# A planner's allowance for a DRAM round trip: softmax row sums in a transformer block on one core

## The chip, the cores and the metric

The kernel runs on one core of one Trainium2 chip. The metric is the device time of one execution, in microseconds (us). The kernel before took 1211.61 us as the median of three runs (1210.0 to 1219.1).

Engine names: PE is the matrix engine, PEld its weight loads, DVE the vector engine, ACT the scalar engine, POOL the general engine. SP only issues DMAs in this kernel, and PSUM holds the outputs of its matmuls (`F_ps`, `S_ps`).

## The reference

```python
x = A_x                                   # (1, 2048, 1024), bf16
h  = x + attention(layernorm(x), wq, wk, wv, wo)   # 32 query heads of 32, ONE key/value head
h2 = h + (sigmoid(g) * u) @ w_down                 # g, u = layernorm(h) @ w_gate, @ w_up; F = 3584
return h2
```

There are 16 tiles of 128 tokens. The exponentials of the scores run on ACT (1024 instructions of 1024 columns, 64 for each token tile). The feed-forward network (FFN) of earlier tiles runs on PE at the same time. For each half of the heads of a tile (32 halves in all), the attention output has to be divided by the row sums of the exponentials.

## The kernel before

The kernel does not write its instruction order by hand. A small list scheduler, `Plan`, simulates all engines with estimated durations. It picks the order of every engine's instructions, and then emits those orders with semaphores. What it believes of a DMA is three lines:

```python
# class Plan, step()  (cut)
        self.free[e] = s + o.occ
        o.start = s
        if o.nbytes:
            if o.pace:
                self.pace_free = s + o.nbytes / self.PACE_RATE
            go = max(s + 1300.0, self.dma_free)
            self.dma_free = go + o.nbytes / self.DMA_RATE      # DMA_RATE = 260.0 bytes per ns
            o.end = self.dma_free + 700.0
        else:
            o.end = s + o.lat
        o.pos = len(self.lists[e])
        self.lists[e].append(o)
```

The row sums make a trip. PE sums over the partitions, DVE takes the reciprocal into `r_sb`, SP writes 8 KB to DRAM (`rd`), and SP reads it back spread over the partitions as 256 KB (`rb`). DVE then multiplies (`OT`).

```python
# mk_SUM(hf), after the summing matmuls  (cut)
rc = pl.op("dve", lambda: DVE.reciprocal(r_sb[:, :], F_ps[:, b, 0:64]), [last, rd_ld.get(hf - 1)], ...)
rd_ld[hf] = dma(lambda: SP.dma_start(r_dram, r_sb[0:P:4, :]), "rd", 8192, [rc, rb_ld.get(hf - 1)], prio=0)
rb_ld[hf] = dma(lambda: SP.dma_start(rb[:, :], bass.AP(r_dram.tensor, r_dram.offset, [[512, 4], [0, DH], [1, 512]])),
                "rb", 262144, [rd_ld[hf], ot_ev.get(hf - 1)], prio=0)
# finish(hf)  (cut)
ot_ev[hf] = pl.op("dve", lambda: DVE.tensor_tensor(out=OT[...], in0=o..., in1=rb[...], op=ALU.mult),
                  [oun_ev[(hf, 1)], op_last.get(c - 1), rb_ld[hf]], prio=0, occ=600, lat=690)
if hh == 1:                                   # second half of the heads: the output projection follows
    for dc in range(2):
        queues["OP"].append(mk_OP(c, dc))
```

All FFN, attention-output and projection matmuls share two PSUM banks (`F_ps`). A bank is free again when DVE has emptied it: `hact` for the FFN, `oun` for the attention output, `h_sb` for the residual sums. DVE also adds up all exponentials (`acc`). The FFN's gate half is emptied by a tanh on ACT (`tnh`).

The softmax here doesn't subtract the row's maximum and nothing guards it: scores larger than these inputs give would overflow.

## Time and profile before

| | before |
|---|---|
| median time | 1211.61 us |
| span of the profiled run | 1210.4 us |
| PE busy / idle (span less busy) | 1110.9 / 99.5 us |
| last score matmul / what follows it | 1120.7 us / 89.7 us |
| DVE idle until the returned sums arrive | 66.6 us in 32 waits |
| one token tile in attention (64 exponentials) | about 68.5 us |

These are two lines of the profile's page of the kernel before. The first gives busy time (share of the span) and instructions of each engine, the second the chain of waits by engine.

```profile
...
PE 1110.9 (92%) x15144; PEld 757.5 (63%) x15176; DVE 869.1 (72%) x1076; ACT 1036.2 (86%) x1159; POOL 51.2 (4%) x93
...
PE 53%; DMA 17%; DVE 14%; ACT 9%; issue 6%; SPq 1%; DVEq 0%
...
```

PE is busy 92% of the span. The chain that ended last still runs through DMAs for 17% of it, and nearly all of that is the row sums' trip (13% for the read, 3% for the write).

The next fence is busy time by window, of the stretch with attention and of the tail after the last score matmul. Columns: window, its length, each engine's busy us (instructions), granted PE clock, DMA share, GB/s.

```profile
...
core 0: us, PE busy (x) PEld busy (x) DVE busy (x) ACT busy (x) POOL busy (x), PEclk, DMA share, GB/s
60.00:1120.70 1060.70, 984.42 (x13461) 650.35 (x13489) 791.95 (x911) 991.42 (x1094) 31.41 (x45) 0.99 0.57 172
1120.70:1210.40 89.70, 83.49 (x1130) 74.53 (x1129) 21.52 (x37) 9.02 (x15) 1.34 (x3) 0.98 0.69 209
...
```

With attention running, PE and ACT are each busy about 93% and DVE 75%. In the tail only PE has much to do.

The waits of the kernel before come next. Columns: engine and line, what it waited for, us in total, times, longest.

```profile
...
engine line waited for: us in total, times, longest us
...
DVE OT L652 <- DMA rb<-r_scratch: 66.6, 32, 6.8
...
ACT Pr L601 <- PE S_ps L367: 55.6, 58, 4.1
...
PE F_ps L367 <- DVE hact L884: 24.5, 26, 3.0
...
PE F_ps L367 <- DVE oun L672: 17.6, 17, 2.8
...
```

DVE stood idle for 66.6 us in front of the multiply (line 652) until the read had landed, once in every half of the heads. PE waited for DVE to empty its banks, and ACT waited for scores.

### The profile page before, as it was taken

The numbers are of one execution on the slowest core, as the hardware profiler recorded it, in microseconds if no ns is written. First come the engines' busy times: TensorE is split into PE (matmuls) and PEld (weight loads), VectorE is DVE, ScalarE is ACT, GpSimd is POOL, SyncE is SP. The second block draws the span as 40 slices with busy tenths as digits, with TensorE's granted clock in tenths as the row PEclk, the third lists the DMA queues.
The fourth block names the chain that finished last, engine by engine and source line by source line (L and its number), as shares of the span: only waits on it lengthen the run. The fifth ranks groups of instructions, "written<-read, shape, count | busy, mean of one in ns | idle before, by whom it ended". The sixth has DMA issues, their size and how long they took to land.

```text
span 1210.4 us, 34593 instructions
## 1 busy us (share of the span) xinstructions
PE 1110.9 (92%) x15144; PEld 757.5 (63%) x15176; DVE 869.1 (72%) x1076; ACT 1036.2 (86%) x1159; POOL 51.2 (4%) x93
## 2 busy tenths in 40 slices
PE   6898978889999999999999999989999999999998
PEld 5533455557566665666666675657665675766797
DVE  8996878667786768687786768677776667777321
ACT  3899999889998999999998999989998998999110
POOL 3200000010000100010000100000000000000000
PEclk9899999999999999999999999999999999999999
DMA  9334284774747375664737384655747374664884
GB/s 314 118 96 150 84 263 138 228 228 149 219 129 213 103 230 150 182 197 138 238 115 228 102 251 142 203 171 165 216 134 221 94 214 131 191 192 123 240 261 128
DMA packets 213335, 214.47 MB, mean 177 GB/s; under 512 B 16192, under 2 KB 199488, under 8 KB 213184
## 3 DMA queue, kind: packets, MB, share of 16 engines
q1 hardware_dynamic: 213184, 212.26, 57.8%
q8 instruction: 119, 1.95, 0.7%
q14 instruction: 32, 0.26, 0.1%
HBM read 204.08 MB, written 8.13 MB: 175 GB/s over the span
## 4 chain that ended last, share of the span: by engine, by line
PE 53%; DMA 17%; DVE 14%; ACT 9%; issue 6%; SPq 1%; DVEq 0%
PE F_ps L367 44%; DMA rb<-r_scratch 13%; ACT Pr L601 8%; PE S_ps L367 8%; DVE acc L578 7%; DMA r_scratch<-r_sb 3%; DVE hact L884 2%; DVE oun L672 1%; DVE st L311 1%; SPq L825 1%; DVE st L313 1%; ACT tnh L878 1%; DVE r_sb L636 1%; PE F_ps L755 0%; DVE OT L652 0%
## 5 line engine op out<-in xcount | busy, mean ns | idle before, releaser
L601 ACT ACTIVATE Pr<-S_ps 128x1024 bf16<-128x1024 f32 x1008 | 965.5, 1034 | 63.2 <-PE S_ps L367 55.6
L578 DVE TENSOR_TENSOR acc<-acc,Pr 128x2048 bf16<-128x2048 bf16 x430 | 525.4, 1222 | 49.9 <-ACT Pr L601 30.7
L367 PE MATMUL F_ps<-hnT,ring 128*128 128x128 bf16 x6752 | 438.9, 220 | 21.9 <-DVE hact L884 8.7
L367 PEld LDWEIGHTS F_ps<-hnT,ring 128*128 128x128 bf16 x6752 | 385.1, 98 | 91.4 <-issue 65.5
L367 PE MATMUL F_ps<-zone,hact 128*128 128x256 bf16 x1792 | 225.8, 273 | 3.0 <-DVE hact L884 2.0
L367 PE MATMUL S_ps<-QTb,kT 32*128 32x512 bf16 x2048 | 204.2, 389 | 15.9 <-ACT Pr L601 12.8
L367 PEld LDWEIGHTS F_ps<-zone,hact 128*128 128x128 bf16 x1792 | 163.7, 98 | 47.8 <-issue 22.8
L367 PE MATMUL F_ps<-Pr,Vt 128*32 128x512 bf16 x2016 | 130.2, 387 | 5.7 <-DVE hact L884 5.5
L878 ACT ACTIVATE tnh<-F_ps 128x512 f32<-128x512 f32 x112 | 67.3, 601 | 71.9 <-PE F_ps L367 63.7
L367 PEld LDWEIGHTS S_ps<-QTb,kT 32*128 32x128 bf16 x2048 | 51.6, 91 | 121.4 <-ACT Pr L601 51.1
L884 DVE SCALAR_TENSOR_TENSOR hact<-tnh,F_ps 128x512 bf16<-128x512 f32 x112 | 76.4, 682 | 39.8 <-PE F_ps L367 36.6
L367 PE MATMUL F_ps<-wo_sb,OT 128*128 128x512 bf16 x234 | 67.1, 416 | 28.1 <-DVE hact L884 7.9
L367 PEld LDWEIGHTS F_ps<-Pr,Vt 128*32 128x32 bf16 x2016 | 46.5, 97 | 64.4 <-issue 21.6
L367 PE MATMUL F_ps<-zone 128*128 128x512 bf16 (+3 forms) x574 | 76.5, 282 | 7.1 <-DVE oun L672 2.8
L676 DVE TENSOR_TENSOR oun<-F_ps,oun 128x512 f32<-128x512 f32 x31 | 21.4, 691 | 75.3 <-PE F_ps L367 75.3
L652 DVE TENSOR_TENSOR OT<-oun,rb 128x512 bf16<-128x512 f32 x31 | 21.5, 693 | 65.4 <-DMA rb<-r_scratch 65.4
L367 PEld LDWEIGHTS F_ps<-zone 128*128 128x128 bf16 x584 | 41.2, 102 | 34.3 <-issue 8.3
L367 PEld LDWEIGHTS F_ps<-wo_sb,OT 128*128 128x128 bf16 x256 | 22.6, 103 | 60.7 <-issue 17.8
L324 POOL TENSOR_SCALAR zb<-mvb 128x1 bf16<-128x1 bf16 (+2 forms) x24 | 12.3, 511 | 1092.5 <-DVE mvb L320 1092.4
L920 DVE SCALAR_TENSOR_TENSOR h_sb<-F_ps,h_sb 128x256 bf16<-128x256 f32 x64 | 26.8, 419 | 25.4 <-PE F_ps L367 25.0
L636 DVE RECIPROCAL r_sb<-F_ps 128x64 f32<-128x64 f32 x32 | 17.8, 558 | 26.3 <-PE F_ps L367 26.3
L578 DVE TENSOR_TENSOR acc<-Pr 128x2048 bf16<-128x2048 bf16 x31 | 36.0, 1163 | 0.0
(70 smaller groups left out, 369.5 us busy)
## 6 DMA issues: line engine op xcount, KB each, us to landing
ring<-in_B_w_gate_dram SPq DMA_DIRECT2D x308, 256.0 KB, 3.8
ring<-in_B_w_up_dram SPq DMA_DIRECT2D x308, 256.0 KB, 3.6
rb<-r_scratch SPq DMA_DIRECT2D x32, 256.0 KB
zone<-in_B_w_down_dram SPq DMA_DIRECT2D x14, 512.0 KB, 4.8
Pr<-in_B_w_up_dram SPq DMA_DIRECT2D x20, 256.0 KB, 4.2
Pr<-in_B_w_gate_dram SPq DMA_DIRECT2D x20, 256.0 KB, 4.7
ring<-in_A_x_dram SPq DMA_DIRECT2D x16, 256.0 KB, 6.1
h_sb<-in_A_x_dram SPq DMA_DIRECT2D x16, 256.0 KB, 3.0
```

What stands on the lines that cost most here:

```text
L311: a = pl.op("dve", lambda s=s, src=src: DVE.bn_stats(st[:, s, 0, :], src[:, 0:512]), dp, prio=prio, occ=600, lat=756, order=[st_user.get(s)])
L313: b = pl.op("dve", lambda s=s, src=src: DVE.bn_stats(st[:, s, 1, :], src[:, 512:1024]), dp, prio=prio, occ=600, lat=756, order=[st_user.ge ...
L324: f = pl.op("pool", lambda: POOL.tensor_scalar(out=zb[:, ph, tk], in0=mvb[:, ph, tk, 1], scalar1=LN_EPS_BF16, scalar2=None, op0=ALU.add), ...
L367: return lambda: PE.matmul(o, lhsT=l, rhs=r, start=start, stop=stop, **kw)
L578: add_op[(hf, kt)] = pl.op("dve", lambda: DVE.tensor_tensor(out=a, in0=in0, in1=slot, op=ALU.add), dp, prio=6, **t_dve(2048, 1.92))
L601: exps[u] = pl.op("act", lambda i=i, pb=pb: ACT.activation(out=slot[:, i * 1024:(i + 1) * 1024].rearrange("p (a b) -> p a b", a=2), in_=S_ ...
L636: rc = pl.op("dve", lambda: DVE.reciprocal(r_sb[:, :], F_ps[:, b, 0:64]), [last, rd_ld.get(hf - 1)], prio=0, occ=64 * 8 / 0.96 + 20, lat=6 ...
L652: ot_ev[hf] = pl.op("dve", lambda: DVE.tensor_tensor(out=OT[:, 4 * hh:4 * hh + 4, :], in0=o.rearrange("p (a b) -> p a b", a=4), in1=rb[:, ...
L676: oun_ev[(hf, 1)] = pl.op("dve", lambda: DVE.tensor_tensor(out=o, in0=F_ps[:, b, :], in1=o, op=ALU.add), [last, oun_ev[(hf, 0)]], prio=0, ...
L878: box["a"] = pl.op("act", lambda: ACT.activation(out=tnh[:, :], in_=F_ps[:, b, :], func=ACTF.Tanh, scale=0.5), [last, box.get("e", ot_ev[1 ...
L884: e = pl.op("dve", lambda: DVE.scalar_tensor_tensor(out=ho, in0=shape(tnh[:, :]), scalar=1.0, in1=shape(F_ps[:, b, :]), op0=ALU.add, op1=A ...
L920: e = pl.op("dve", lambda: DVE.scalar_tensor_tensor(out=h_sb[:, t % 4, sl], in0=F_ps[:, b, 0:DW], scalar=0.5, in1=h_sb[:, t % 4, sl], op0= ...
```

## The change

The intent is to tell the planner the truth about the trip, so that it no longer places the multiply on DVE before the sums can be back. The description also named the tanh output and a hold of the first FFN pass. The diff contains nothing of those; this is all of it:

```diff
     ENG = ("act", "dve", "pool", "sp")
     DMA_RATE = 260.0
+    LATE = {"rd": 1500.0, "rb": 3500.0}
     PACE_RATE = 250.0
...
             go = max(s + 1300.0, self.dma_free)
             self.dma_free = go + o.nbytes / self.DMA_RATE
-            o.end = self.dma_free + 700.0
+            o.end = self.dma_free + 700.0 + self.LATE.get(o.key, 0.0)
```

The two numbers shift every later decision of the planner, so the orders of PE, ACT, DVE and SP all change. The set of instructions stays the same, except that three casts move from DVE to ACT and a few weight loads go to other buffers.

## The prediction

> **What the diff is.** Two constants of the planner: the write of the softmax reciprocals to DRAM is assumed to land 1.5 us later, the broadcast read back 3.5 us later. Nothing in it touches the tanh output or a hold on the first FFN pass, which the description names; I predict the diff. By the two instruction orders the work is the same (three casts move from DVE to ACT); only its order on PE, ACT, DVE and SP differs.
>
> **What bounds it now.** Until the last score matmul at 1120.7 us PE and ACT together; then PE alone for 89 us (timeline). In the table of 50 us windows from 300 to 1100 us PE is busy 47 of 50 us, ACT 46.8, DVE 37. Idle between 50 and 1110 us (gaps in the trace): PE 78 us, ACT 69 us.
>
> **The wait aimed at.** From the end of the reciprocal to the multiply that uses the returned sums takes 6.5 to 13 us, once 19 (timeline). The planner allowed about 5 us plus queueing, and DVE keeps its program's order: it stands still for 66.6 us in 32 waits (waits view: OT on rb, at most 6.8 us). Behind it stand the evacuations that free PE's two banks: PE waited 24.5 us for hact and 17.6 us for oun. In the stretches from each such wait to 6 us after its multiply (287 us in all) lie 54.5 of PE's 94 us idle and 56 us of ACT's; at the rate elsewhere PE would have had about 12. So some 42 us of PE idle belong to these waits.
>
> [...]here the small write took 1.7 to 4.4 us to land and the read about 4.7 to 9 us, so the trace decides. The new allowance, about 10 us, matches the measured trip.
>
> **What the new order does.** DVE work between reciprocal and multiply, priced with traced durations, rises from typically 5.4 to 11 us to 10 to 15 us: the 66.6 us of waits should fall under 20 us, ACT's idle from 69 to about 30 us. One token tile (64 exponentials) now takes 68.5 us on average; back to back, ACT needs 62 us (0.92 us spacing, seven tanh at 0.48) and PE is busy 63.6. I expect 65 to 66 us: 15 tiles give back 38 to 52 us.
>
> **What it costs.** The new plan puts less FFN work under attention: after the last score matmul PE has 960 gate/up and 351 down matmuls instead of 729 and 308, an estimated 18 us more at traced spacings (57 and 107 ns). So attention shortens by about 46 us and the tail grows by about 17: net 29 us.
>
> **Prediction: 1182 us**, 1165 to 1203 with 8 in 10. Chances: faster by over 2% 0.62, within 2% 0.35, slower 0.03.
>
> **What would show it.** Right: OT's wait on rb under 20 us; PE's waits on hact and oun halved; last score matmul near 1075 us; tail near 106 us; busy times unchanged within 1%. Wrong, step one: rb waits remain, since the read is issued later on SP, behind paced weight loads. Step two: waits go, but PE's idle returns elsewhere (oun copies now stand right behind the multiply). Step three: the longer tail starves for weights (waits on ring or Pr loads over 5 us).
>
> **What would make it wrong.** PE and ACT are so evenly loaded that relieving one leaves the other's limit: tiles at 67 us would leave about 1205.

The sum is attention shorter by about 46 us and a tail longer by about 17, so 29 us net, from about 1211 to 1182 us. Its traced spacings of 57 and 107 ns are 56 and 109 ns as medians of the tail in the trace of the kernel before.

## More of the kernel before

The timeline shows one such wait in the kernel before. Columns: start, duration, engine, line, operation, output<-inputs, form, count, and in brackets the idle time before it and what ended it.

```profile
...
956.20 0.56 DVE L636 RECIPROCAL r_sb<-F_ps 128x64 f32<-128x64 f32 x1 [2.65 <-PE F_ps L367]
...
956.79 0.49 SPq L638 DMA_DIRECT2D r_scratch<-r_sb  x1
...
960.39 0.55 SPq L639 DMA_DIRECT2D rb<-r_scratch  x1
...
963.58 0.40 PE L367 MATMUL S_ps<-QTb,kT 32*128 32x512 bf16 x4
...
963.91 0.29 PE L367 MATMUL F_ps<-hnT,ring 128*128 128x128 bf16 x2
...
965.45 0.69 DVE L652 TENSOR_TENSOR OT<-oun,rb 128x512 bf16<-128x512 f32 x1 [3.49 <-DMA rb<-r_scratch]
966.06 0.68 DVE L884 SCALAR_TENSOR_TENSOR hact<-tnh,F_ps 128x512 bf16<-128x512 f32 x1
...
966.80 2.79 PE L367 MATMUL F_ps<-hnT,ring 128*128 128x128 bf16 x30 [2.60 <-DVE hact L884]
...
969.52 0.61 PE L367 MATMUL S_ps<-QTb,kT 32*128 32x512 bf16 x4
...
970.06 2.30 PE L367 MATMUL F_ps<-Pr,Vt 128*32 128x512 bf16 x32
...
```

The reciprocal ends at 956.76. The write is issued at once, the read at 960.39, and the multiply starts at 965.45 after DVE has been idle for 3.49 us. Behind the multiply in DVE's order stands `hact`, which empties a bank, so PE idles 2.60 us before 966.80. The last two lines show something that the prediction did not use: the four score matmuls take 0.61 us where they took 0.40 just before. The window of this trouble shows the same in its clock column (next fence, busy time by window of the kernel before: clock 0.97).

```profile
...
950.00:1000.00 50.00, 47.14 (x703) 34.27 (x692) 32.12 (x35) 45.29 (x52) 0.00 (x0) 0.97 0.54 161
...
```

## The result, and the profile after

| | before | after |
|---|---|---|
| median time, the runs when the prediction was made | 1212.76 us (1210.0 to 1219.1) | 1163.85 us (1163.70 to 1163.99) |
| ratio | | 0.959, 95% interval 0.9551 to 0.9628 |
| span of the profiled run | 1210.4 us | 1161.9 us |
| PE idle | 99.5 us | 62.7 us |
| lost to half clock | 19.1 us | 5.1 us |
| last score matmul / tail | 1120.7 / 89.7 us | 1058.4 / 103.5 us |

A ratio is the mean time of one kernel's fast runs over that of the other's fast runs of the same rounds, so it is not quite the ratio of the medians quoted. "Lost to half clock" is half of the time that the trace's clock records show at a granted clock of 0.5. That it is half is an estimate, from the gate and up matmuls of the kernel before: they start every 107 ns at that clock and every 56 elsewhere.

The same two lines of the page of the kernel after:

```profile
...
PE 1099.2 (95%) x15146; PEld 755.7 (65%) x15176; DVE 866.6 (75%) x1073; ACT 1032.4 (89%) x1162; POOL 42.6 (4%) x93
...
PE 79%; DVE 10%; ACT 8%; issue 3%; DMA 0%; DVEq 0%
...
```

The DMAs have left the chain altogether (0%); PE makes up 79% of it.

Busy time by window of the kernel after, the stretch with attention and the tail:

```profile
...
60.00:1058.40 998.40, 957.22 (x13182) 631.29 (x13207) 786.08 (x903) 984.71 (x1093) 22.88 (x45) 1.00 0.59 180
1058.40:1161.90 103.50, 99.17 (x1403) 91.08 (x1403) 24.75 (x43) 11.21 (x18) 1.34 (x3) 1.00 0.69 214
...
```

ACT is now busy 98.6% of the attention stretch, PE 95.9%. The tail is longer because the new order leaves more FFN work for it (1403 matmuls in that window instead of 1130).

The waits of the kernel after (line numbers are one higher):

```profile
...
ACT Pr L602 <- PE S_ps L368: 6.7, 24, 1.4
...
PE F_ps L368 <- DVE hact L885: 4.7, 7, 1.2
...
PE F_ps L368 <- DVE oun L673: 4.0, 8, 0.7
...
DVE OT L653 <- DMA rb<-r_scratch: 0.5, 1, 0.5
...
```

The wait for the sums fell from 66.6 to 0.5 us, PE's waits for `hact` and `oun` fell from 42.1 to 8.7 us, and ACT's wait for scores from 55.6 to 6.7 us.

One trip in the timeline of the kernel after:

```profile
...
874.40 0.56 DVE L637 RECIPROCAL r_sb<-F_ps 128x64 f32<-128x64 f32 x1 [1.12 <-PE F_ps L368]
...
875.62 0.49 SPq L639 DMA_DIRECT2D r_scratch<-r_sb  x1
...
880.96 0.56 SPq L640 DMA_DIRECT2D rb<-r_scratch  x1
...
885.98 0.68 DVE L885 SCALAR_TENSOR_TENSOR hact<-tnh,F_ps 128x512 bf16<-128x512 f32 x1
...
886.43 0.56 PEld L368 LDWEIGHTS F_ps<-hnT,ring 128*128 128x128 bf16 x10 [0.23 <-issue]
...
887.72 0.68 DVE L653 TENSOR_TENSOR OT<-oun,rb 128x512 bf16<-128x512 f32 x1
...
888.07 0.40 PE L368 MATMUL S_ps<-QTb,kT 32*128 32x512 bf16 x4
...
888.40 1.05 PE L368 MATMUL F_ps<-Pr,Vt 128*32 128x512 bf16 x16
...
```

The trip itself has not become shorter: reciprocal to multiply now takes 12.8 us. But DVE has no idle time before the multiply, `hact` runs ahead of it, and the four score matmuls take 0.40 us. Busy time by window, the same 50 us as above: clock 1.00.

```profile
...
950.00:1000.00 50.00, 48.56 (x669) 32.01 (x669) 38.98 (x46) 49.36 (x55) 1.34 (x3) 1.00 0.63 193
...
```

### The profile page after: what moved, and what is told of

Read it like the earlier page. It is cut to its first block, busy times and chain, and to the rows that moved or that the text cites. A ratio compares the mean times of both kernels' runs of the same rounds, so it can differ in the third digit from the quotient of the medians.

```text
span 1161.9 us, 34615 instructions
## 1 busy us (share of the span) xinstructions
PE 1099.2 (95%) x15146; PEld 755.7 (65%) x15176; DVE 866.6 (75%) x1073; ACT 1032.4 (89%) x1162; POOL 42.6 (4%) x93
## 4 chain that ended last, share of the span: by engine, by line
PE 79%; DVE 10%; ACT 8%; issue 3%; DMA 0%; DVEq 0%
PE F_ps L368 66%; PE S_ps L368 12%; ACT Pr L602 8%; DVE acc L579 3%; DVE st L312 1%; DVE st L314 1%; ACT tnh L879 1%; PE F_ps L756 1%; DVE zone L253 1%; DVE r_sb L637 0%; DVE hnT L762 0%; DVE ring L344 0%; DVE oun L673 0%; DVE oun L677 0%; DVE zone L351 0%
## 5 line engine op out<-in xcount | busy, mean ns | idle before, releaser
L368 PE MATMUL S_ps<-QTb,kT 32*128 32x512 bf16 x2048 | 203.1, 387 | 14.7 <-ACT Pr L602 14.2
L368 PEld LDWEIGHTS S_ps<-QTb,kT 32*128 32x128 bf16 x2048 | 51.5, 91 | 121.6 <-ACT Pr L602 56.9
L368 PE MATMUL F_ps<-wo_sb,OT 128*128 128x512 bf16 x236 | 60.6, 381 | 6.3 <-DVE h_sb L921 2.5
L368 PEld LDWEIGHTS F_ps<-zone 128*128 128x128 bf16 x584 | 40.9, 101 | 32.1 <-issue 6.8
L325 POOL TENSOR_SCALAR zb<-mvb 128x1 bf16<-128x1 bf16 (+2 forms) x24 | 6.4, 268 | 1039.1 <-DVE mvb L321 1038.9
L579 DVE TENSOR_TENSOR acc<-Pr 128x2048 bf16<-128x2048 bf16 x31 | 36.1, 1165 | 0.0
L736 DVE TENSOR_TENSOR h_sb<-F_ps,h_sb 128x512 bf16<-128x512 f32 x32 | 22.0, 687 | 9.1 <-PE F_ps L368 8.9
```

Of the source, the lines that this page charges most:

```text
L368: return lambda: PE.matmul(o, lhsT=l, rhs=r, start=start, stop=stop, **kw)
L579: add_op[(hf, kt)] = pl.op("dve", lambda: DVE.tensor_tensor(out=a, in0=in0, in1=slot, op=ALU.add), dp, prio=6, **t_dve(2048, 1.92))
L736: h_ev[(t, dc)] = pl.op("dve", lambda: DVE.tensor_tensor(out=h_sb[:, t % 4, sl], in0=F_ps[:, b, :], in1=h_sb[:, t % 4, sl], op=ALU.add), [ ...
```

## The experiments

Thirteen runs were made: eleven new kernels, and the kernel after and the best of the new ones once more. Each stood beside the kernel before on the same chip. Theory W says that DVE's waits for the sums are the cost. They idle PE and ACT, and PE's idle stretches bring on stretches at half clock (the clock records of the kernel before show a granted clock of 0.5 in eleven stretches of 3.41 us and one that the end of the trace cuts off). Its rival R says that the new orders are better for another reason (less FFN work under attention, or a lucky draw of the planner).

### The wait taken away in the order of the kernel before

```diff
-  in1=rb[:, :].rearrange(...), op=ALU.mult)      # OT
+  in1=o.rearrange(...), op=ALU.mult)             # same work, data already there; wrong result on purpose
...
+  # after planning: OT's dependence on the read is dropped; SP waits for the last read at the end
```

> The order of the kernel before, untouched, but the multiply reads a tile that is already there instead of the returned sums (the result is wrong on purpose; both DMAs still run). Theory W (the waits of DVE for the sums are the cost: they idle PE and ACT, and PE's idle stretches bring on stretches at half clock): no wait on rb, PE's idle between 50 and 1110 us down from 78 to 30-45 us, at most 4 half-clock stretches instead of 12, time 1150 to 1172 us. Rival R (the new order itself is better balanced, it has less FFN work under attention): the waits are worth less than half of the gain, time 1190 to 1210 us.

Measured: 1150.15 us against 1204.91, ratio 0.955 (0.9506 to 0.9594). PE's idle between 50 and 1110 us fell to 29 us, one microsecond below the range expected. Three half-clock stretches were left, at 45 us, at 219 us and in the last microseconds. Busy time by window:

```profile
...
60.00:1062.10 1002.10, 975.36 (x13482) 646.53 (x13481) 789.03 (x910) 986.04 (x1094) 31.48 (x45) 1.00 0.60 182
1062.10:1147.90 85.80, 81.73 (x1131) 73.71 (x1129) 21.44 (x37) 9.00 (x15) 1.34 (x3) 1.00 0.70 218
...
```

The order of the kernel before, with nothing moved, gives slightly more than the whole gain once DVE need not wait. R falls. Its tail is also 17.7 us shorter than that of the kernel after (85.8 against 103.5), so the new order is not better balanced. It costs about 14 us (1164 against 1150), and the change pays that price to be rid of the waits.

The control does the same to the kernel after, where no wait is left to take.

> Control for the kernel that took the wait away: the order of the kernel after, the multiply again reads a tile that is already there (wrong result on purpose). There is nothing left to take away, so both theories: 1160 to 1166 us, as the kernel after. If reading another tile helped by itself, it would be 1155 us or less.

Measured: 1164.01 us, as the kernel after. Reading another tile does not help by itself.

### The multiply put back early in the order of the kernel after

```diff
+  # after planning: on DVE alone, each OT moves up to 4 additions earlier,
+  # never ahead of anything that it depends on through any engine's order
```

> The order of the kernel after, but each multiply stands up to 4 additions earlier on DVE; the other engines' orders untouched. W: waits on rb of 40 to 90 us come back, with at least 5 half-clock stretches, time 1190 to 1220 us. R: the balance of the other engines is kept, so 1164 to 1180 us.

Measured: 1351.03 us, ratio 1.122: the right direction, but far outside the range. The waits of this kernel:

```profile
...
DVE OT L653 <- DMA rb<-r_scratch: 146.9, 32, 8.0
...
PE F_ps L368 <- DVE hact L885: 90.0, 22, 6.4
...
```

The waits came back at more than twice the size of before (146.9 us). Part of that is SP's order, which had not been moved with it: it has weight loads between write and read, so the read is issued 4.5 us after the write at the median, where it was 3.4 us in the kernel before. Besides, the edit went further than the order of the kernel before: in the second half of the heads DVE has 5.5 us of work between reciprocal and multiply at the median, where the kernel before had 7.6. How the excess divides between the two was not traced. PE spent 54 times 3.41 us at half clock after the first 60 us, half of which is 92 us. The experiment confirms where the cost sits, but its size is not that of the kernel before.

### Another draw of the planner without the allowance

```diff
-SWITCH = 97.0
+SWITCH = 107.0      # kernel before; LATE not added
```

> The planner of the kernel before with another constant moved (the cost of a change of PE mode, 97 to 107 ns): every engine's order is drawn anew, with less FFN work under attention as in the kernel after, but the multiplies stay as early. W: waits on rb of 45 to 75 us, time 1195 to 1225 us. R, or a mere lucky draw in the kernel after: 1160 to 1190 us.

`SWITCH` is the planner's own constant; no run here measures what a change of PE mode takes.

Measured: 1224.99 us, ratio 1.015 (1.0077 to 1.0218), just inside the range of W. Its tail has 886 gate and up and 336 down matmuls, which is between the kernel before (729 and 308) and the kernel after (960 and 351). Every engine's order differs from before, but the wait is still there:

```profile
...
DVE OT L652 <- DMA rb<-r_scratch: 61.6, 30, 4.0
...
```

This one new draw gained nothing by itself.

### Half of the waits removed

```diff
+  # kernel before, after planning: on DVE alone, the OT of the first half of the heads
+  # of each token tile (hf even, from 2 on) moves up to 4 additions later
```

> The order of the kernel before, but only the multiplies of the first half of the heads of each token tile (which no output projection awaits) stand up to 4 additions later on DVE. W: waits on rb fall from 67 to about 35 us and the time by 18 to 32 us, to 1180 to 1195 us. R: 1205 to 1215 us.

Measured: 1185.64 us, ratio 0.984 (0.9795 to 0.9887).

```profile
...
DVE OT L652 <- DMA rb<-r_scratch: 35.4, 18, 5.5
...
```

Waits of 66.6 us became 35.4, and the time fell by 19 us of the 55 that all waits are worth. In the trace the first half's waits fell from 34.9 to 3.3 us, and the second half's stayed (31.7 and 32.1). That would make the second half, where the output projection follows the multiply, the dearer one, unless moving the multiplies cost something by itself; no run here separates the two.

### The allowance halved and doubled

```diff
-    LATE = {"rd": 1500.0, "rb": 3500.0}
+    LATE = {"rd": 750.0, "rb": 1750.0}       # half;   double: {"rd": 3000.0, "rb": 7000.0}
```

> The change at half size: 0.75 us for the write, 1.75 us for the read. Its order keeps as much FFN work under attention as the kernel before (758 gate/up and 308 down matmuls after the last score matmul). Theory W: waits on rb of 12 to 35 us. If each microsecond of wait costs alike (about 55 us for 67), 1162 to 1180 us with half-clock stretches in proportion; if short waits leave PE's clock alone, at most 4 stretches and 1152 to 1165 us. Rival (only the allowance that fits the measured trip helps): over 1185 us.

Measured: 1175.56 us, ratio 0.968 (0.961 to 0.9746).

```profile
...
PE F_ps L368 <- DVE h_sb L921: 15.8, 11, 3.3
...
DVE OT L653 <- DMA rb<-r_scratch: 13.3, 12, 3.9
...
```

The wait fell to 13.3 us, as expected, and five half-clock stretches after the first 60 us were left, more than the four of the milder guess. But 15.8 us of PE's idle is a wait for `h_sb`, which the kernel before had only at 2.8 us. The order itself brought a new wait. The rival's range, over 1185 us, was not reached.

> The change at double size: 3 us and 7 us. No waits on rb (under 1 us). W together with the cost of displaced work: after the last score matmul PE has 1231 gate/up and 560 down matmuls, some 138 us by the traced spacings against 99 in the kernel after, so 1180 to 1205 us, though attention itself is as fast. Rival (a longer allowance is only safer): 1160 to 1170 us.

Measured: 1234.52 us, ratio 1.017, and the wait is gone (0.0 us), with a tail of 167.7 us. The rival "a longer allowance is only safer" is not borne out. The range was missed by 30 us. The trace shows PE idle for 121.6 us and 23.9 us lost to half clock, against 62.7 and 5.1 in the kernel after: idle time and half clock also come without the wait for the sums. The largest of PE's waits is one for exponentials on ACT, 37.0 us against 14.2. The result was also wrong (relative error 0.26). This order runs part of the FFN for two token tiles at once (matmuls of 256 columns), a path that neither kernel compared here takes. Whether that path has an error was not pursued.

### A version that should beat both: one miss, one hit

```diff
-    LATE = {"rd": 1500.0, "rb": 3500.0}
+    LATE = {"rd": 750.0, "rb": 1750.0}
...
+  # after planning: on DVE alone, OT of the first half of the heads up to 2 additions later
```

> A version that should beat both: the half-size allowance, whose order has little FFN work left for the tail, and on DVE alone the multiplies of the first half of the heads up to 2 additions later. W: waits on rb under 10 us, at most 3 half-clock stretches, 1147 to 1162 us, the time of the wrong-on-purpose kernel without waits.

Measured: 1174.35 us. This missed.

```profile
...
PE F_ps L368 <- DVE h_sb L921: 15.3, 11, 3.1
...
DVE OT L653 <- DMA rb<-r_scratch: 11.6, 9, 3.8
...
```

The waits that were left in the half-size version sat in the second half of the heads, so moving the first half could not help, and the wait for `h_sb` stayed. Then the extra time was given to the read alone, with a different value for each half of the heads:

```diff
-    LATE = {"rd": 1500.0, "rb": 3500.0}
+    LATE = (3500.0, 5000.0)               # first and second half of the heads
...
-            o.end = self.dma_free + 700.0 + self.LATE.get(o.key, 0.0)
+            o.end = self.dma_free + 700.0 + (self.LATE[o.tag % 2] if o.key == "rb" else 0.0)
...
+                rb_ld[hf].tag = hf
```

> A search for a version that beats the kernel after: extra time for the read alone, 3.5 us for the first half of the heads and 2.5 us for the second. DVE work between reciprocal and multiply is 9.8 and 11.1 us, the order leaves 800 gate/up and 324 down matmuls for after the last score matmul. Ledger of the runs so far: time = about 1095 us of PE work + PE's idle + half of the time at half clock. With waits on rb under 10 us, idle 50 to 62 us and at most 4 half-clock stretches: 1150 to 1164 us. If idle comes from other orders' waits as in h_even2: 1165 to 1178 us.

> The same search, 3.5 us for the first half of the heads and 5 us for the second: DVE work 9.8 and 12.9 us, the same work left for the tail (800 and 324 matmuls). Waits on rb under 5 us; 1148 to 1162 us by the ledger, 1165 to 1178 us if other waits take their place.

> The same search, 2.5 us and 3.5 us: DVE work 8 and 12.5 us, the least work left for the tail (755 and 308 matmuls). Some waits on rb come back in the first half of the heads, 5 to 15 us, which cost little there (b_half: 31 us of them were worth 19 us). 1152 to 1168 us.

Measured, in this order: 1158.16, 1155.53 and 1157.22 us, with waits on the read of 0.0, 0.0 and 3.4 us. All were correct and inside their ranges of time. The last had less wait than the 5 to 15 us said. All three keep the waits away and leave less work for the tail than the kernel after (tails of 93.7, 92.9 and 88.0 us). The best one was timed once more, on the same chip as the kernel after.

> The searched version (3.5 us and 5 us) on the same chip as the kernel after: 1154 to 1157 us, 0.6 to 0.9% under the kernel after. If the difference was one of chips, within 0.3% of it.

Measured: 1154.24 us against 1163.71 us for the kernel after. The ratios to the kernel before of the same rounds are 0.958 (0.9553 to 0.9611) and 0.966 (0.9631 to 0.969). This version beats both kernels, by 0.8% over the kernel after.

### What the half clock costs, with the order held fixed

> The kernel after once more, for its time on the same chip as many runs of the kernel before. If the missing term is half clock, runs of the kernel before lie on a line of time against the time lost to the clock (span times one minus mean granted clock) with a slope of 0.9 to 1.3, and carried to the lost time of the kernel after (about 5 us) that line gives 1188 to 1200 us, so that 25 to 35 us of the gain are left for idle alone, as the prediction's sum had it. If half clock only accompanies the waits, the slope is under 0.5 or there is no line. The kernel after itself: 1163 to 1165 us.

The kernel after took 1163.71 us. Nine runs of the kernel before on this chip had spans of 1198.7 to 1206.8 us at mean granted clocks of 0.991 to 0.982. A line through them gives 0.79 us of span for each microsecond lost to the clock (correlation 0.89), and at 5 us lost a span of 1195 us. The slope is a little below the range expected, but its standard error is 0.15, and the line is carried beyond its data (10.8 to 21.7 us lost). PE's idle time may vary along with the clock in these runs, so the line does not isolate the clock. On three other chips, with seven runs each, it was 1.06, 1.07 and 0.77 (the last with a correlation of only 0.5). So the order of the kernel before, at the clock of the kernel after, would take about 1195 us by this estimate. Some 33 us of the gain are then left for idle time, and about 10 us (on this chip) to 14 us (in the profiled run) are the clock.

The runs together give a ledger. PE work is PE's busy time less what half clock lost.

| kernel | wait for sums | PE idle | lost to half clock | PE work | span |
|---|---|---|---|---|---|
| before | 66.6 | 99.5 | 19.1 | 1091.8 | 1210.4 |
| after | 0.5 | 62.7 | 5.1 | 1094.1 | 1161.9 |
| before, wait taken away | 0.0 | 48.2 | 3.6 | 1096.1 | 1147.9 |
| before, half moved | 35.4 | 76.0 | 15.4 | 1096.4 | 1187.7 |
| other draw | 61.6 | 102.9 | 27.3 | 1097.6 | 1227.8 |
| half allowance | 13.3 | 72.7 | 11.9 | 1087.8 | 1172.4 |
| 3.5 and 5 us, again | 0.2 | 56.5 | 3.4 | 1094.0 | 1153.9 |

PE work is the same within 1% in all of them. The kernel with the multiply put back early is left out, since its PE work comes to 1069.5 us in this sum: PE stood idle in 47.9 of its 187.7 us at half clock, and that idle time lost nothing. Counted for the busy part alone, it is 1093.5 us, in line with the others. What differs is idle time and half clock, and they go together.

## Why the prediction was wrong

The mechanism was right and the size was too small: 1182 us (1165 to 1203) was predicted and 1163.85 us measured, a gain of 49 us where 29 were forecast.

- **The wait: right.** It fell from 66.6 to 0.5 us ("under 20" was said), and the experiments with the wait taken away, halved and put back tie the time to it.
- **PE's waits on hact and oun: right**, and more than halved (42.1 to 8.7 us).
- **The cost: nearly right.** The tail was predicted at 106 us and is 103.5.
- **The step that failed: "So attention shortens by about 46 us".** The last score matmul came at 1058.4 us instead of the 1075 expected, so attention shortened by 62.3 us. One term of that sum was missing: time at half clock. The prediction took PE's busy time as fixed ("busy times unchanged within 1%"), and it fell by 11.7 us, a little over 1%. Up to the last score matmul, half clock cost the kernel before about 17 us (ten stretches of 3.41 us, half of each lost) and the kernel after 5.1 us (three), some 12 of the 16 us that were missed. From 200 us on, all eight stretches before the last score matmul of the kernel before came at a PE idle stretch; the kernel after has none after 170 us.
- **The rest of the miss is idle time.** Of the 46 us, 18 were FFN work moved to the tail, which left 28 for idle. The sum of PE's gaps up to the last score matmul fell by 35 us (93.3 to 58.4). The estimate of a tile at 65 to 66 us left room for a loss that did not remain; most tiles took 64 to 65. The prediction had itself found 42 us of PE idle at these waits, but its sum used only 28; 42 and the 18 of moved work would have given 60. Measured, the 62.3 us are 34.9 of idle, about 12 of half clock and about 15 of work moved to the tail.
- **The feared limits did not bind.** ACT, at 98.6% busy, took the work; weights did not starve the tail (PE was busy for 99.2 of its 103.5 us).

That idle stretches bring on the half clock is not shown by itself here. The traces show what fits it: the clock records hold only 0.5 and 1.0, and the stretches at 0.5 last 3.41 us, save those that the end of the trace cuts off. Each of the eight stretches named above began within 0.7 us of the end of a PE gap. After PE's first matmul no gap in the kernel before is longer than 3.05 us. In the stretches at half clock of the kernel before, the gate and up matmuls start every 107 ns instead of every 56. What a run here shows by itself is that idle stretches and half clock occur together, and for how long; the clock was never switched while idle was held fixed.

The slopes of four chips, 0.77 to 1.07, differ by no more than the scatter of so few runs (standard errors of 0.15 to 0.6), so they do not settle what a microsecond lost to the clock costs. The wrong result at the doubled allowance is open.

## What to carry to other kernels

Where a scheduler orders in-order engines, measure every long latency that it assumes. An instruction placed a few microseconds before its data can be there holds up everything behind it (66.6 us of waits on DVE in the kernel before; without them the same order took 1150.15 us instead of 1204.91), and a wrong order of the rest may cost less than that. Allow no more than the trip needs: too much pushes work into a tail where little overlaps with it (a tail of 103.5 us with the allowance of the change, 88.0 to 93.7 with the three smaller ones). When pricing PE's idle stretches, add the half-clock stretches that come with them (19.1 us lost beside 99.5 us of idle in the kernel before, 5.1 beside 62.7 in the kernel after); look at the clock records as well as the gaps.

## What the traces show of gaps, clock and DMAs

- PE was idle for 2.03 us before 424.3 us in the kernel before, and a stretch at half clock began at 424.8 us. A gap of 2.69 us before 661.9 us in the same run was followed by none. So it was for three of the run's eleven gaps over 2 us after the first 50 us: the length of a gap alone did not decide here.
- The half clock cost 19.1 us of 1210.4 us in the profiled run of the kernel before (by the estimate above). Runs of this program spread over 8 us (1200.49 to 1208.63 on one chip), where the kernel after, with one gap over 2 us after the first 50 us of its profiled run, stayed within 1 us (1163.38 to 1164.24).
- The read, issued by SP, which spreads 8 KB from DRAM over 128 partitions under the traffic of the other loads, took 4.7 to 9 us from issue until the waiting multiply could start in the kernel before.
- The two DMAs of the trip, one after the other in one queue, were separated by what the program's order put between their issues: 4.4 us between the issues of write and read at the median in the kernel after, 3.4 us in the kernel before, where the write had landed after 2.7 us.
